# First batch entry's attention: exponentials transposed by TensorE, values with a column of ones, inputs loaded ahead

## The chip, the cores and the metric

The kernel runs on one NeuronCore of a Trainium2 chip. The metric is the device time of one execution in microseconds (us); of the kernel before, three runs were taken. The engines are named as the profile names them: PE (TensorE's matrix products) and PEld (its weight loads), DVE (VectorE), ACT (ScalarE), POOL (GpSimd) and SP (SyncE, which here only issues DMA transfers).

## What is computed

Windowed attention over 8 batch entries, 8 heads, 576 positions and 64 columns a head, and then a gated two-layer MLP on the 4608 tokens.

```python
scores = scale * np.matmul(q, k.transpose(0, 1, 3, 2))
rel = pos[:, None] - pos[None, :]
mask_plain = (rel >= 0) & (rel < window)                                   # window = 32
mask_dil = (rel >= 0) & (rel < window * dilation) & (rel % dilation == 0)  # dilation = 4
masks = np.stack([mask_plain if h < H // 2 else mask_dil for h in range(H)], axis=0)
scores = np.where(masks[None, :, :, :], scores, -1000000000.0)
attn = np.exp(scores - np.max(scores, axis=-1, keepdims=True))
attn = attn / (np.sum(attn, axis=-1, keepdims=True) + 1e-09)
x = np.matmul(attn, v)              # then (tokens, heads * columns) = (4608, 512)
h = x @ w_in                        # (512, 2048)
out = (h * (1.0 / (1.0 + np.exp(-1.702 * h)))) @ w_out
```

## The kernel before, in words

The MLP is done in nine groups of 512 tokens: one for the first 512 positions of each batch entry (`main`, tiles with `_m_` in their names) and one for the 64 positions that are left of all eight (`rest`). In a group, the 2048 hidden columns come in 16 blocks of 128. For block f, `up(f)` forms the hidden block on PE (12 products of 128x512, line 522), ACT takes a tanh (line 530), DVE multiplies the gate (line 533; called "gate f" below), and `down(f)` adds the block's share to four output banks (12 products, lines 558 to 562). Each operand is split into a high and a low fp32r part, and three products stand for one.

The weights lie in memory as 64-bit numbers. `decode(n)` brings one block of w_in or w_out (n = 0 to 31, even n for w_in, odd n for w_out) from there: a load of 512 KB into one of five cells (line 244), two ACT passes (lines 245, 246), one for the sign on ACT or DVE (238 or 240), two DVE passes (248, 250), a copy to the high part (ACT or DVE, lines 197 and 199) and a subtraction to the low part (DVE or POOL, line 204). All 32 blocks are decoded while the first main group runs.

A batch entry's attention is done in four head pairs k (k = 0 to 3 are the first entry, 4 to 7 the second). For a pair: `scores` (lines 328 and 337: the mask goes in by a product with the identity, then 76 products of 32 queries by up to 64 keys), `softmax` (lines 342 to 400: maximum, subtraction and exponential, sum, reciprocal, multiplication by it, a transposition of 32x32 blocks by DVE into `ct`, and eight copies of `ct` blocks into the banded tile `bt` by ACT, DVE or a DMA), `product` (line 414: `bt` by the values, 18 products whose result has the columns on the partitions), and `drain_x` (line 446 and on), which splits the result into `xh` (ACT) and `xl` (DVE), which `up` needs for all four pairs.

The order on each engine is fixed ahead of the run. All work is entered with `add(costs, urgency, work, reads, writes)`, and `Plan.ordered` places it by a list schedule: it takes the engine that can start first, on it the ready operation of lowest urgency, and the cheapest engine that may do it. Each engine then works through its list strictly in that order, and so does SP's queue of DMA issues. In the first 30 us of its own reckoning the plan fills PE's idle time with products of the identity (`warm`, line 630).

## Time and profile before

| | us |
|---|---|
| median of three runs | 918.69 (917.89 to 919.01) |
| the profiled execution, its own time | 920.26 |
| span of its profile | 918.5 |
| PE busy | 882.0 |
| DVE busy | 520.6 |
| ACT busy | 322.1 |
| POOL busy | 38.3 |

The profile is one execution; times in it count from the span's start. A share of the span mixes two stages: an early one, in which attention of the first entry and the decoding of the weights run, and a long one after it. A row of the timeline reads: start, duration, engine, line, operation, written tile <- read tiles, count, and in brackets how long the engine stood idle before and what ended that. A row of the table of stretches reads: stretch, its length, then busy time of PE, PEld, DVE, ACT and POOL (with instructions), the granted clock of PE as a share, the busy share of the DMA engines, GB/s.

### The profile page before, as it was taken

To read this page: it belongs to the slowest core of one execution; us is meant where nothing else is said; L and a number is where in the kernel's file an instruction comes from. 1 tells how busy PE (TensorE), PEld (TensorE's weight loads), DVE (VectorE), ACT (ScalarE), POOL (GpSimd) and SP (SyncE) were. 2 spreads that over 40 slices of the span, in tenths; PEclk is the share of its full clock that TensorE was granted. 3 is DMA by queue.
4 is the path that set the end of the run, shared out by engine and by line. 5 is a ranking of instruction groups with operands and counts; after the bars stand their busy time and mean duration, and the time that the engine had idled before them with its cause. 6 is when DMAs were issued, how large, how long until landed. Compare 5 with 4: busy or idle time off the path is not lost.

```text
span 918.5 us, 16806 instructions
## 1 busy us (share of the span) xinstructions
PE 882.0 (96%) x7096; PEld 718.5 (78%) x7096; DVE 520.6 (57%) x1004; ACT 322.1 (35%) x590; POOL 38.3 (4%) x40
## 2 busy tenths in 40 slices
PE   5679999999999999999999999999999999999997
PEld 2457778888888888888888888888888888888885
DVE  4878898676567636763667347654733433343332
ACT  2877887433344114321443134312421221121111
POOL 1121201000000000000000000000000000000000
PEclk9889999999999999999999999999999999999999
DMA  8566773323041102310222012300100010001002
GB/s 203 135 193 181 251 225 99 119 64 89 3 133 51 47 1 91 92 46 1 91 72 68 0 46 92 92 1 1 66 1 1 1 46 1 1 1 47 0 1 46
DMA packets 38683, 61.96 MB, mean 67 GB/s; under 512 B 20176, under 2 KB 20176, under 8 KB 38608
## 3 DMA queue, kind: packets, MB, share of 16 engines
q1 hardware_dynamic: 38608, 60.90, 22.1%
q8 instruction: 55, 0.90, 0.4%
q14 instruction: 20, 0.16, 0.1%
HBM read 49.81 MB, written 9.44 MB: 64 GB/s over the span
## 4 chain that ended last, share of the span: by engine, by line
PE 89%; DMA 4%; DVE 2%; ACT 2%; issue 0%; SPq 0%; ACTq 0%
PE hp_m L522 36%; PE acc_m L558 12%; PE acc_m L562 12%; PE acc_m L559 12%; PE hp_r L522 5%; PE av L414 4%; PE sp L337 3%; PE acc_r L562 2%; PE acc_r L558 2%; PE acc_r L559 2%; DMA cell<-wo_dram 1%; DMA qk<-qk_dram 1%; DMA bt<-ct 1%; DMA cell<-wi_dram 1%; ACT cell L238 0%
## 5 line engine op out<-in xcount | busy, mean ns | idle before, releaser
L522 PE MATMUL hp_m<-xh,wih 128*128 128x512 f32 x512 | 201.7, 394 | 7.1 <-DVE g_m L533 3.6
L533 DVE SCALAR_TENSOR_TENSOR g_m<-g_m,hp_m 128x512 f32<-128x512 f32 x128 | 87.8, 686 | 212.6 <-ACT g_m L530 211.9
L558 PE MATMUL acc_m<-gh,woh 128*128 128x512 f32 x512 | 201.0, 393 | 1.3 <-ACT gh L197 1.2
L522 PE MATMUL hp_m<-xh,wil 128*128 128x512 f32 x512 | 200.2, 391 | 0.7 <-DVE wil L204 0.7
L522 PE MATMUL hp_m<-xl,wih 128*128 128x512 f32 x512 | 200.1, 391 | 0.0
L559 PE MATMUL acc_m<-gh,wol 128*128 128x512 f32 x512 | 199.4, 389 | 0.0
L530 ACT ACTIVATE g_m<-hp_m 128x512 f32<-128x512 f32 x128 | 76.6, 598 | 308.2 <-PE hp_m L522 304.9
L562 PE MATMUL acc_m<-gl,woh 128*128 128x512 f32 x512 | 142.6, 391 | 0.0
L522 PEld LDWEIGHTS hp_m<-xh,wih 128*128 128x128 f32 x512 | 96.6, 189 | 29.5 <-DVE g_m L533 4.9
L558 PEld LDWEIGHTS acc_m<-gh,woh 128*128 128x128 f32 x512 | 96.1, 188 | 22.3 <-ACT gh L197 1.6
L522 PEld LDWEIGHTS hp_m<-xh,wil 128*128 128x128 f32 x512 | 96.6, 189 | 20.9 <-DVE wil L204 1.0
L522 PEld LDWEIGHTS hp_m<-xl,wih 128*128 128x128 f32 x512 | 96.5, 188 | 20.5
L562 PEld LDWEIGHTS acc_m<-gl,woh 128*128 128x128 f32 x512 | 95.7, 188 | 20.2
L559 PEld LDWEIGHTS acc_m<-gh,wol 128*128 128x128 f32 x512 | 96.1, 188 | 19.6
L204 DVE TENSOR_TENSOR gl<-g_m,gh 128x512 fp32r<-128x512 f32 x125 | 88.6, 709 | 15.7 <-ACT gh L197 7.2
L197 ACT ACTIVATE bt<-ct 32x320 f32<-32x320 f32 x109 | 51.1, 469 | 34.8 <-DVE ct L381 33.0
L199 DVE CAST gh<-g_m 128x512 fp32r<-128x512 f32 x106 | 45.3, 427 | 9.0 <-PE acc_m L559 0.5
L533 DVE SCALAR_TENSOR_TENSOR g_r<-g_r,hp_r 128x512 f32<-128x512 f32 x16 | 11.0, 688 | 54.4 <-ACT g_r L530 54.4
L197 ACT ACTIVATE xm<-av 128x512 f32<-128x512 f32 (+2 forms) x42 | 23.1, 613 | 52.9 <-PE av L414 35.0
L371 ACT ACTIVATE pr<-pr 128x640 f32<-128x640 f32 x32 | 23.7, 740 | 48.5 <-DVE pr L204 48.4
L199 DVE COPY bt<-ct 32x320 f32<-32x320 f32 x107 | 34.0, 318 | 2.4
L530 ACT ACTIVATE g_r<-hp_r 128x512 f32<-128x512 f32 x16 | 9.6, 598 | 73.4 <-PE hp_r L522 73.4
(129 smaller groups left out, 873.0 us busy)
## 6 DMA issues: line engine op xcount, KB each, us to landing
qk<-qk_dram SPq DMA_DIRECT2D x17, 576.0 KB, 5.1
out_dram<-ost_m SPq DMA_DIRECT2D x32, 256.0 KB, 2.1
second<-qk_dram SPq DMA_DIRECT2D x13, 576.0 KB, 4.7
v<-vp_dram SPq DMA_DIRECT2D x34, 216.0 KB, 4.5
cell<-wi_dram SPq DMA_DIRECT2D x11, 512.0 KB, 4.9
cell<-wo_dram SPq DMA_DIRECT2D x11, 512.0 KB, 4.0
words<-vp_dram SPq DMA_DIRECT2D x24, 216.0 KB, 4.2
second<-wi_dram SPq DMA_DIRECT2D x5, 512.0 KB, 5.1
```

Of the source, the lines that this page charges most:

```text
L197: A.activation(dst, src, AF.Copy, scale=scale)
L199: V.tensor_copy(out=dst, in_=src)
L204: (V if e == DVE else G).tensor_tensor(out=dst, in0=a, in1=b, op=op)
L337: T.matmul(dst[:, w:w + n], u["q"][rows, 32 * g:32 * g + 32], keys[:, at:at + n], start=not masked(k), stop=True, tile_position=(D * a, 32 ...
L371: add({ACT: 0.75}, urgency, lambda e: A.activation(pr, pr, AF.Exp, scale=0.125), (), (PR,))
L414: T.matmul(dst, u["v"][a][0:KW, m], bt[0:KW, a, m], start=True, stop=True, skip_group_check=True)
L522: T.matmul(hps[f], st[:, f, c], mv[:, c], start=c == 0 and k == 0, stop=c == NC - 1 and k == 2)
L530: A.activation(self.g32, hps[f], AF.Tanh, scale=0.851)
L533: V.scalar_tensor_tensor(out=self.g32, in0=self.g32, scalar=1.0, in1=hps[f], op0=ALU.add, op1=ALU.mult)
L558: T.matmul(self.acc[j], woh[:, f, cols], gh, start=f == 0, stop=False)
L559: T.matmul(self.acc[j], wol[:, f, cols], gh, start=False, stop=False)
L562: T.matmul(self.acc[j], woh[:, f, P * j:P * j + P], self.g[f][1], start=False, stop=f == NF - 1)
```

## The change

Only the first entry's four pairs (k = 0 to 3) are done in another way, and the plan's rules around them.

- Both heads' scores go to one bank, so maximum and subtraction are one DVE instruction of 640 columns each (before: two of 320 each). The exponentials are no longer summed, scaled or transposed by DVE. PE transposes them by products with a float identity (`exact`): ten products into `turned` and a spare bank (`turn`). ACT copies them to `ct`.
- PE multiplies `ct` by overlapping blocks of 64 values with a column of ones behind them (65 columns, 40 products, `times_values`). The last column is the sum. It is copied out, gets 1e-9 added and is inverted; DVE multiplies the 64 columns by it while it takes them out of the bank (two instructions), and PE transposes the result back (`turn_back`, five products). Then `drain_x` as before.
- The values of the first entry come as `vb`, one load of 128x1170 floats (585 KB) a pair in place of two of 216 KB. Queries, keys and values of the four pairs have places of their own (`bt`, `second`, `xm`, `xr`, `cell2`); the clearing of `bt` comes after that.
- In the plan: operations of the first entry that can start within 0.6 of another operation's cost go ahead of it (`AHEAD`), the first weights' loads go among the entry's loads, `up(1)` of the first group gets a bank of its own, and the `warm` products use another bank.

```diff
+            if e != DMA and ops[i][1][0] >= soon:
+
+                cost = min(abs(ops[i][0][k]) for k in ops[i][0])
+                near = [j for j in open_[e] if 0.0 <= ops[j][1][0] < soon and start(j, e) < when + AHEAD * cost]
+                if near:
+                    i = min(near, key=lambda j: (start(j, e), ops[j][1]))
+                    when = start(i, e)
...
-        early = ("pr0",) if n in (1, 2) else ()
-        add({DMA: 524}, urgency, lambda e: load(raw, src), early, (R, R + "l", *taken))
+        add({DMA: 524}, {0: -5.0, 1: -2.0}.get(n, urgency), lambda e: load(raw, src), (), (R, R + "l", *taken))
...
-        add({DMA: 590}, 1.6 * k - 2.0, work, waits(k), (place,))
+        add({DMA: 590}, (-9.0, -8.0, -6.0, -3.0)[k] if k < NC else 1.6 * k - 2.0, work, waits(k), (place,))
...
+                flat = (None, late, main_x, left_x)[k] if k else temp([P, nb], F32, "v", f"v_{k}")
+                u["v"] = flat[:, 0:nb].rearrange("p (g d) -> p g d", g=NB)
+                load(flat[:, 0:nb], vb[k])
...
     def first_attention(k, urgency):
...
-        softmax(k, urgency)
-        add({PE: 1.1}, urgency - 1.0e5, lambda e: product(k), (lots(k)[1], *(f"bt.{m}" for m in range(8))),
-            ("hp" if k % 2 else "av", f"spare{k}"))
+        exponentials(k, urgency)
+        def turn(e):
...
+            for t in range(QT):
+                n = min(P, S - P * t)
+                for a in range(2):
...
+                    T.matmul(dst, pr[0:n, a, t], exact[0:n, 0:n], start=True, stop=True, tile_position=(0, D * a),
+                             skip_group_check=True)
+        add({PE: 1.3}, urgency - 1.0e5, turn, (PR,), ("acc0", f"end{y}"))
+        add({ACT: 0.62}, urgency, lambda e: copy(e, ct[:, 0:GT], u["turned"]), ("acc0",), (CT + ".0", f"x{y}.0", f"x{y}.1"))
+        add({ACT: 0.22, DVE: 0.15}, urgency, lambda e: copy(e, ct[:, GT:], u["end"]), (f"end{y}",), (CT + ".1", f"x{y}.0", f"x{y}.1"))
+        def times_values(e):
...
+                    T.matmul(u["sums"][a][32 * j:32 * j + 32, t], ct[rows, 32 * g:32 * g + 32], u["v"][rows, g],
+                             start=True, stop=True, tile_position=(D * a, 32 * j), skip_group_check=True)
...
+            add({DVE: 0.17, ACT: 0.2}, urgency, lambda e, a=a: copy(
+                e, sm[:, a], u["sums"][a][:, :, D]), (f"acc{2 + a}",), (f"{SM}.{a}",))
...
+            add({DVE: 0.48}, urgency, lambda e, a=a: pair(
+                e, x[:, :, a], u["sums"][a][:, :, 0:D], sm[:, a, :, None].broadcast_to([P, QT, D]), ALU.mult),
+                (f"acc{2 + a}", SM, CT + ".0", CT + ".1"), (f"x{y}.{a}",))
+        def turn_back(e):
...
+                T.matmul(u["av"][:, P * t:P * t + n] if t < QT - 1 else u["rest"],
+                         x[0:n, t].rearrange("p a w -> p (a w)"), exact[0:n, 0:n], start=True, stop=True,
+                         skip_group_check=True)
...
-            place = "hp"
+            place = "sp" if self is main[0] and f == 1 else "hp"
...
+    keys = [f"bt.{m}" for m in range(8)]
+    add({POOL: 1.2}, 20.0, lambda e: G.memset(bt[0:KW], 0.0), (), ("first qk1", *keys))
```

**DVE between the second pair's `xl` and the third's.** Names: `pr`, `sm` are exponentials and sums of a pair, `words` and the cells belong to `decode`, `sums` is the new product's bank; line 250 of before is line 267 of after. Before:

```order
L250 ISA words<-cell_115,words 128x1024
L381 STREAM_TRANSPOSE ct_84<-pr_78 128x320 x2
L204 TENSOR_TENSOR xl<-av_408,xh 128x512
L199 COPY bt<-ct_84 32x10x32 x3
L372 TENSOR_REDUCE sm_83<-pr_79 128x10
L248 TENSOR_SCALAR words<-words 128x512
L373 TENSOR_SCALAR sm_83<-sm_83 128x10
L204 TENSOR_TENSOR wil<-words,wih 128x512
L376 RECIPROCAL sm_83<-sm_83 128x10
L250 ISA words<-cell_116,words 128x1024
L204 TENSOR_TENSOR pr_79<-pr_79,sm_83 128x320 x2
```

And after:

```order
L267 ISA words<-cell_118,words 128x1024
L222 TENSOR_TENSOR xl<-av_498,xh 128x512
L217 COPY ct_85<-spare 128x64
L520 TENSOR_SCALAR sm_82<-sm_82 128x10
L522 RECIPROCAL sm_82<-sm_82 128x10
L222 TENSOR_TENSOR ct_84<-sums_0_509,sm_82 128x5x64
L222 TENSOR_TENSOR ct_84<-sums_1_510,sm_82 128x5x64
L267 ISA words<-cell_116,words 128x1024
L265 TENSOR_SCALAR words<-words 128x512
L217 CAST woh<-words 128x512
L222 TENSOR_TENSOR xl<-av_571,xh 128x3x128
```

The sums (line 372), the transpositions (381) and the copies to `bt` (199) are gone from DVE; the second pair's `xl` now stands behind the decoding of a block in `cell_118`.

**PE around the start of the first group's products.** `hp_m_0` and `hp_m_1` are the banks of `up(0)` and `up(1)`, `av` a pair's result. Before, from the last pair's `product` on:

```order
L414 MATMUL av_527<-bt,xr 64x64
L414 MATMUL av_527<-bt,cell_117 64x64
L414 MATMUL idle<-bt,xr 64x64
L414 MATMUL idle<-bt,cell_117 64x64
L522 MATMUL hp_m_0_569<-xh,wih 128x512
L522 MATMUL hp_m_0_569<-xh,wil 128x512
L522 MATMUL hp_m_0_569<-xl,wih 128x512
```

And after, from the end of the second pair's `times_values` on:

```order
L512 MATMUL sums_1_422<-second,ct_85 32x65
L594 MATMUL hp_m_0_475<-xh,wih 128x512
L594 MATMUL hp_m_0_475<-xh,wil 128x512
L594 MATMUL hp_m_0_475<-xl,wih 128x512
L497 MATMUL turned_482<-early,pr_79 64x128 x8
L497 MATMUL spare<-early,pr_79 64x64 x2
L533 MATMUL av_498<-early,ct_85 128x128 x4
L533 MATMUL spare<-early,ct_85 128x64
```

The first group's products now begin between the pairs, and nine of the twelve of `up(1)` stand ahead of the last three of `up(0)`.

**SP's queue of loads at the start.** `qk`, `bt`, `second`, `xm`, `xr` and `cell` are the places that the loads fill. Before:

```order
L279 DMA xm<-qk_dram 128x1152
L297 DMA second<-vp_dram 96x576
L297 DMA xr<-vp_dram 96x576
L297 DMA xm<-vp_dram 96x576
L297 DMA xr<-vp_dram 96x576
L244 DMA cell_115<-wi_dram 128x512
L297 DMA xr<-vp_dram 96x576
L297 DMA cell_117<-vp_dram 96x576
L279 DMA qk_180<-qk_dram 128x1152
L395 DMA bt<-ct_84 32x10x32 x2
L244 DMA cell_116<-wo_dram 128x512
```

And after:

```order
L294 DMA second<-qk_dram 128x576
L295 DMA xm<-qk_dram 128x576
L261 DMA cell_116<-wi_dram 128x512
L312 DMA second<-vb_dram 128x1170
L294 DMA xr<-qk_dram 128x576
L295 DMA cell_118<-qk_dram 128x576
L261 DMA cell_117<-wo_dram 128x512
L312 DMA xm<-vb_dram 128x1170
L312 DMA xr<-vb_dram 128x1170
L261 DMA cell_116<-wo_dram 128x512
L261 DMA cell_118<-wi_dram 128x512
```

The first w_in block's load moved ahead of the second pair's values, the last pair's queries and keys no longer wait for the first pair's buffer, and the `bt` transfers are gone.

More of the change, by code (lines that the diff above doesn't have):

```diff
@@ L273, in work @@
         def work(e):
-            flat = {"qk0": None, "qk1": late, "qk2": main_x}[place]
-            if flat is None:
-                flat = temp([P, 2 * nq], F32, "qk", f"qk_{k}")
+            if k in (2, 3):
+                u["q"] = (late if k == 2 else left_x)[:, nb:nb + nq]
+                u["k"] = main_x[:, nb:nb + nq] if k == 2 else cell[:, 0:nq]
+                load(u["q"], qk[k, :, 0])
+                load(u["k"], qk[k, :, 1])
+                return
+            flat = windows if k == 1 else late if place == "qk1" else temp([P, 2 * nq], F32, "qk", f"qk_{k}")
             u["q"], u["k"] = flat[:, 0:nq], flat[:, nq:2 * nq]
@@ L297, in work @@
                 load(u["v"][a][0:KW], vp[k, :, a])
-        add({DMA: 442}, 1.6 * k - 0.3, work, waits(k), (place,))
+        add({DMA: 600 if k < NC else 442}, (-7.0, -4.0, -1.0, 0.0)[k] if k < NC else 1.6 * k - 0.3, work, waits(k),
+            (place,))
     def waits(k):
@@ L397, in work @@
                     copy(e, dst, src)
-            costs = ({DMA: 82} if NC <= k < FIRST * NC or k < NC and m % 4 == 3 else {ACT: 0.49, DVE: -0.33})
+            costs = {DMA: 82} if k < FIRST * NC else {ACT: 0.49, DVE: -0.33}
             add(costs, urgency, work, (f"{CT}.{prev}",), (f"bt.{m}",))
@@ L403, in product @@
         u = pairs[k]
-        u["av"] = bank([P, GT], "hp" if k < NC and k % 2 else "av", f"av_{k}")
-        if k < NC:
-            u["rest"] = spare_bank()[:, 1, LT * k:LT * k + LT]
-        else:
-            sp = pairs[k + 1]["sp"] if k + 1 < len(pairs) else bank([P, 2, GT], "sp", f"sp_{k + 1}")
-            u["rest"] = sp[:, 1, QT * W:QT * W + LT]
+        u["av"] = bank([P, GT], "av", f"av_{k}")
+        sp = pairs[k + 1]["sp"] if k + 1 < len(pairs) else bank([P, 2, GT], "sp", f"sp_{k + 1}")
+        u["rest"] = sp[:, 1, QT * W:QT * W + LT]
         for m in range(NW):
@@ L416, in spare_bank @@
     def spare_bank():
-        if not misc:
-            misc["bank"] = bank([P, 2, GT], "sp", "idle")
-        return misc["bank"]
+        if "spare" not in misc:
+            misc["spare"] = bank([P, GT], "acc1", "spare")
+        return misc["spare"]
     def drain_x(k, urgency):
         u, (b, c) = pairs[k], divmod(k, NC)
-        freed = ("qk2", "v2") if b == 1 else ()
+        freed = ("first v2", "first qk2") if b == 1 else ()
         def view(x):
@@ new lines, in first_attention @@
+        add({PE: 1.0}, urgency - 1.0e5, times_values, (lots(k)[1], CT + ".0", CT + ".1"), ("acc2", "acc3"))
+        x = cts[y].rearrange("p h a t q -> p (h a t q)").rearrange("p (t a w) -> p t a w", t=QT, a=2)
+        for a in range(2):
+            add({DVE: 0.17, ACT: 0.2}, urgency, lambda e, a=a: copy(
+                e, sm[:, a], u["sums"][a][:, :, D]), (f"acc{2 + a}",), (f"{SM}.{a}",))
+        add({DVE: -0.15}, urgency, lambda e: V.tensor_scalar(
+            out=sm, in0=sm, scalar1=1.0e-9, scalar2=None, op0=ALU.add), (f"{SM}.0", f"{SM}.1"), (SM,))
@@ new lines, in first_attention @@
+        add({DVE: 0.19}, urgency, lambda e: V.reciprocal(out=sm, in_=sm), (), (SM,))
+        for a in range(2):
+            add({DVE: 0.48}, urgency, lambda e, a=a: pair(
+                e, x[:, :, a], u["sums"][a][:, :, 0:D], sm[:, a, :, None].broadcast_to([P, QT, D]), ALU.mult),
+                (f"acc{2 + a}", SM, CT + ".0", CT + ".1"), (f"x{y}.{a}",))
+        def turn_back(e):
+            u["av"] = bank([P, GT], "av", f"av_{k}")
+            u["rest"] = spare_bank()[:, LT * (2 + k):LT * (3 + k)]
+            for t in range(QT):
+                n = min(P, S - P * t)
+                T.matmul(u["av"][:, P * t:P * t + n] if t < QT - 1 else u["rest"],
+                         x[0:n, t].rearrange("p a w -> p (a w)"), exact[0:n, 0:n], start=True, stop=True,
+                         skip_group_check=True)
@@ L475, in attention @@
             add({PE: 1.2}, urgency - 1.0e5, lambda e: scores(k), (lots(k)[0],),
-                ("sp", *(f"spare{j}" for j in range(NC))), 1.0)
+                ("sp",), 1.0)
         load_v(k)
@@ L628, in warm @@
     def warm(e):
-        if 0 not in main[0].hps and "sp" not in pairs[NC]:
-            T.matmul(spare_bank()[:, 0], ident, ident[:, None, :].broadcast_to([P, GT // P, P]), start=True, stop=True)
-    for work, e in plan.ordered(warm, WARM):
+        if 0 not in main[0].hps:
+            if "idle" not in misc:
+                misc["idle"] = bank([P, GT], "hp", "idle")
+            T.matmul(misc["idle"], ident, ident[:, None, :].broadcast_to([P, GT // P, P]), start=True, stop=True)
+    for work, e in plan.ordered(warm, WARM, NC):
         work(e)
@@ L652 @@
     vp[:, :, 32:] = order(v)
+    vb = np.ones((H, D, NB, DV), v.dtype)
+    vb[:, :, :, :D] = np.stack([vp[0, :, 32 * g:32 * g + D] for g in range(NB)], axis=2)
     vp = np.stack([vp[:, :, D * m:D * m + KW] for m in range(NW)], axis=2)
```

114 lines of the change are left out of this document (66 added, 48 removed).

## The prediction

> **What bounds the kernel now.** I read the table of stretches first, to see where PE stands idle.
>
> ```profile
> 0.00:20.00 20.00, 9.03 (x239) 4.83 (x240) 7.04 (x22) 3.48 (x5) 2.37 (x10) 1.00 0.90 209
> 20.00:54.84 34.84, 22.32 (x272) 14.07 (x270) 28.40 (x68) 28.35 (x51) 3.42 (x4) 0.80 0.63 173
> 54.84:119.09 64.25, 59.83 (x634) 47.40 (x634) 54.89 (x106) 50.62 (x77) 13.93 (x10) 1.00 0.67 205
> 119.09:155.25 36.16, 34.24 (x252) 27.95 (x252) 32.68 (x64) 30.92 (x52) 3.04 (x2) 1.00 0.54 159
> 155.25:175.25 20.00, 20.00 (x191) 16.50 (x190) 15.21 (x31) 9.11 (x18) 2.02 (x2) 1.00 0.38 127
> ```
>
> The last row is the long stage: PE busy 20.00 of 20, nothing else can shorten it. All that can be won lies ahead of it. There DVE and ACT are the full engines, not PE: in the second row 28.40 and 28.35 of 34.84. The edges of the rows are three of the sixteen "gates" of the first main group (line 533), which the timeline gives, with the first product of `up(0)`:
>
> ```profile
> 49.32 0.76 PE L522 MATMUL hp_m<-xh,wih 128*128 128x512 f32 x1 [3.07 <-DVE xl L204]
> 54.84 0.69 DVE L533 SCALAR_TENSOR_TENSOR g_m<-g_m,hp_m 128x512 f32<-128x512 f32 x1
> 155.25 0.68 DVE L533 SCALAR_TENSOR_TENSOR g_m<-g_m,hp_m 128x512 f32<-128x512 f32 x1
> 140.42 2.72 PE hp_m L522 x12
> ```
>
> The next rows price PE's attention: busy PE and count of line 414 (36 products), then of line 337 (76), in one stretch at full clock, and the two mask products.
>
> ```profile
> 23.00:26.60 3.60, 1.27 (x36) 1.13 (x36) 1.00 0.74 174
> 23.00:26.60 3.60, 1.00 (x76) 0.84 (x76) 1.00 0.74 174
> 23.75 0.43 PE L328 MATMUL sp_acc<-mask,ident 128*128 128x320 bf16 x2
> ```
>
> PE starts when the last `xl` is there. Twelve products take 2.72 at full pace (the row from the chain of waits). From gate 0 to gate 15 PE has 348 products to do (348 x 2.72 / 12 = 78.9 us) and the second entry's attention (four times 1.00 + 0.43 for scores and mask, 1.27 for the product: 10.8): 89.7, and takes 100.4. So some 10.7 us are lost there too, while DVE and ACT together work 169.1 of 200.8. From 20 us to gate 15 the two do 225.9 us of work in 135.25 us, 1.67 us a us. I take this sum of two engines' work as what sets gate 15; after it the order is the same.
>
> **What the change removes and adds on DVE and ACT.** The groups of 0 to 50 us:
>
> ```profile
> L197 ACT ACTIVATE bt<-ct 32x320 f32<-32x320 f32 x11 | 5.2, 468 | 0.3
> L199 DVE COPY bt<-ct 32x320 f32<-32x320 f32 x13 | 4.1, 317 | 0.3
> L362 DVE TENSOR_REDUCE mx<-sp_acc 128x5 f32<-128x320 f32 x8 | 3.8, 481 | 10.9 <-PE sp_acc L337 10.9
> L204 DVE TENSOR_TENSOR pr<-sp_acc,mx 128x320 f32<-128x320 f32 x8 | 3.8, 485 | 0.1
> L381 DVE STREAM_TRANSPOSE ct<-pr 128x320 f32<-128x320 f32 x8 | 3.6, 491 | 0.0
> L372 DVE TENSOR_REDUCE sm<-pr 128x10 f32<-128x640 f32 x4 | 3.3, 818 | 0.1
> L204 DVE TENSOR_TENSOR pr<-pr,sm 128x320 f32<-128x320 f32 x5 | 2.7, 567 | 0.0
> L197 ACT ACTIVATE xh<-av 128x512 fp32r<-128x512 f32 x2 | 1.2, 598 | 1.0 <-PE av L414 0.8
> 27.00 0.22 ACT L197 ACTIVATE xr<-idle 128x64 f32<-128x64 f32 x1
> 56.24 0.82 DVE L368 TENSOR_REDUCE mx<-sp 128x10 f32<-128x640 f32 x1
> 57.10 0.82 DVE L204 TENSOR_TENSOR pr<-sp,mx 128x640 f32<-128x640 f32 x1
> ```
>
> Gone are the first seven rows: 26.5 us. Maximum and subtraction come back as eight instructions of 0.82 (last two rows): 6.6. The multiplication by the inverse comes back as eight instructions of 128x320 out of a bank; nearest is the subtraction, 485 ns: 3.9. New are four copies of 128x512 out of a bank (598 ns: 2.4), four of 128x64 (0.22: 0.9) and eight of the sums, five columns each (at most 0.22, at least nothing: 1.8 or 0; I take 1.8, the row of the nearest size). Together 15.6. Net 10.9 us less; with the sums' copies at nothing it is 12.7.
>
> The rest comes from what the plan then gives to POOL. Up to gate 15 the order of after holds on DVE 16 low-part subtractions of weights for 22, 13 of `gl` for 12, 15 high-part casts for 19 (ACT 17 for 13), and 4 multiplications `pr<-pr,sm` for 8 in the second entry.
>
> ```profile
> L204 DVE TENSOR_TENSOR wol<-words,woh 128x512 fp32r<-128x512 f32 x10 | 6.9, 686 | 0.1
> L204 DVE TENSOR_TENSOR gl<-g_m,gh 128x512 fp32r<-128x512 f32 x12 | 8.4, 698 | 2.3 <-ACT gh L197 2.3
> L199 DVE CAST woh<-words 128x512 fp32r<-128x512 f32 x9 | 3.8, 417 | 0.1
> L197 ACT ACTIVATE woh<-words 128x512 fp32r<-128x512 f32 x5 | 3.2, 643 | 0.0
> ```
>
> That is -6 x 0.686 + 0.698 - 4 x 0.417 + 4 x 0.643 - 4 x 0.567 = -4.8. Its cover is POOL, busy 13.93 of 64.25 in the third stretch. Sum -15.7 us of work; over 1.67 that is **9.4 us earlier at gate 15**. What a block costs the two engines:
>
> ```profile
> L245 ACT ACTIVATE words<-cell 128x512 f32<-128x512 f32 x16 | 10.8, 677 | 3.0 <-DMA cell<-wo_dram 1.6 <-DMA cell<-wi_dram 0.8 <-DVE wol L204 0.6
> L246 ACT ACTIVATE cell<-cell 128x512 uint32<-128x512 uint32 x16 | 10.7, 678 | 2.4 <-DMA cell<-wi_dram 1.5 <-DMA cell<-wo_dram 0.8
> L238 ACT ACTIVATE cell<-cell 128x512 f16<-128x512 f32 x15 | 20.6, 1374 | 0.2
> L250 DVE CUSTOM_DVE_ANT_0 words<-cell,words 128x1024 uint16<-128x1024 uint16 x17 | 11.5, 676 | 0.0
> ```
>
> By gate 0 the queues hold 10.9 less but one more decoded block (six of line 250 for five): 0.68 + 0.68 + 1.37 + 0.68 and a cast of 0.42, 3.8. The 7.1 left, over the second stretch's own 1.63 us a us, is 4.3: gate 0 near 50.5. PE then has 94.9 us to gate 15 for 89.7 less the nine products of `up(1)` that already stand ahead (2.0): it fits.
>
> **PE.** It loses four times 18 products and gains 10 transposes of up to 128 columns, 40 products of 65 and 5 transposes back a pair. At half clock, line 414 in a later stretch:
>
> ```profile
> 43.90:46.30 2.40, 1.98 (x32) 1.82 (x32) 0.50 0.39 70
> ```
>
> That is 0.062 a product for 0.035 (1.27 / 36). The bounds at full clock: a transpose between 0.07 (two 64-column products) and 0.23 (a 512-column one, 2.72 / 12); a product of 65 between 0.013 (1.00 / 76) and 0.035. A pair then costs 1.6 to 4.9 in place of 1.27; I take 2.5, since each transpose fills only a quarter of 512 columns. It lies in PE's idle 12.5 us of the second stretch and costs nothing; without that cover four pairs would cost 1 to 15.
>
> The granted clock matters for that:
>
> ```profile
> 40.00:42.00 2.00, 0.00 (x0) 0.00 (x0) 1.97 (x6) 1.98 (x3) 0.00 (x0) 0.50 0.29 117
> 52.00:54.00 2.00, 2.00 (x7) 1.39 (x5) 1.45 (x3) 1.37 (x3) 0.00 (x0) 0.67 0.93 303
> 18.90 5.01 PE L630 MATMUL idle<-ident 128*128 128x512 bf16 x14
> 27.27 2.10 PE L630 MATMUL idle<-ident 128*128 128x512 bf16 x9 [0.69 <-ACT xr L197]
> ```
>
> After PE's idle time around 40 the clock is 0.50 and returns only during 52 to 54, four us after the products began at 49.32. The filling products ran at 0.36 each from 18.90 and at 0.23 from 27.27. The change takes out nearly all of them (40 become 4 in the order). [...]
>
> **Loads.** The values grow by 153 KB a pair, 0.63 MB together, ahead of the weights.
>
> ```profile
> 14.00:16.00 2.00, 1.13 (x63) 0.91 (x63) 0.00 (x0) 0.62 (x1) 0.00 (x0) 1.00 1.07 229
> 18.45 0.53 PE L337 MATMUL sp_acc<-xm 64*32 64x64 f32 x13 [2.43 <-issue]
> 21.06 0.67 ACT L245 ACTIVATE words<-cell 128x512 f32<-128x512 f32 x1 [6.44 <-DMA cell<-wi_dram]
> 24.38 0.33 PE L337 MATMUL sp_acc<-qk 64*32 64x32 f32 x14 [0.20 <-DMA qk<-qk_dram]
> ```
>
> In the first 20 us the DMA engines are full at 229 GB/s, so 0.63 MB is 2.8 us for what stands behind. The first w_in block landed at 21.06; it now has 2.9 MB up to its end instead of 3.6 ahead in the queue and lands some 3 us sooner. The last pair's scores began at 24.38, with PE waiting only 0.20 for them: "all at once" gives little. In the later stretches DMA is busy 0.54 to 0.67, which hides the 2.8; uncovered, it costs 2.8. POOL's moved clearing of `bt` waits for a read of it and nobody waits on POOL then.
>
> **Sum.** The profiled execution took 920.26 (span 918.5 and 1.76 around it): 920.26 - 9.4 = 910.9. The median of the runs is 1.57 lower, so I predict **909.3**.
>
> **Rivals.**
>
> *PE's floor.* If the lead on DVE and ACT also ends the 10.7 us lost after gate 0 (at gate 10 the order has three pairs' softmax behind it in before, two after), gate 15 comes 4.3 + 10.7 + 2.0 = 17 us earlier: 901.7. Against it: the two engines would have to do 1.8 us a us, which only the fourth stretch (1.76) came near. 0.13.
>
> *Late inputs.* The lists are fixed, and first-pair work stands behind weights that may land late: ACT's second exponential behind the first w_in block, the second pair's `xl` on DVE behind `cell_118`, whose load is the sixteenth or so in a full queue (6.9 MB: 33 us at 229 GB/s, and 3 more as the 21.06 row lagged). If half the gain goes in such waits: 914. For it: 6.44 above, and the 2.43 in which PE had nothing to execute that the trace shows. 0.17.
>
> *Half clock.* A pair at half clock costs 1.6 to 4.9 more, and one pair, the last, is on the path; 24 products of `up(0)` and `up(1)` at 0.43 for 0.23 cost 4.8, of which before pays 2. In all 4.4 to 7.7 on 909.3: 913.7 to 917.0, about 915. [...] Against it: PE's list is dense from about 25 us on, which restored the clock in 52 to 54. 0.08.
>
> *Nothing moves.* The gates wait for something that the change leaves as it is. A load's landing ended only 0.20 at PE above. 0.05, 918.7.
>
> *Slower: the weights' loads become the bound.* If each block is late by the extra 2.8 us and the wait is not caught up, the time is 918.7 + 2.8 = 921.5. It decides from the point where ACT's waits for landed cells (lines 245 and 246 above, 55 to 155 us: 1.6 + 0.8 + 1.5 + 0.8 = 4.7) grow by more than the 9.4 won. A DMA share of 0.67 speaks against it. 0.07.
>
> **The numbers.** The forecast, 6 to 12 us better, has 0.50. Faster by over 0.2% (1.8 us, about what a measurement of this kernel can tell from no change) is the forecast and the first three rivals: 0.88; within it 0.05; slower 0.07. The range leaves out the slower end and no change, and the outer half of the PE floor: 901 to 917.
>
> **What would show it.** Right: line 372 four times fewer and no DVE transposes before gate 0; gate 0 near 50.5, gate 15 near 146, DVE and ACT still near 1.67 us a us between, PE saturated after it. Wrong: ACT idle on `cell` for over 10 us before gate 0 (late inputs); `hp_m` products at 0.43 beyond 24 of them, or a clock of 0.50 past 50 us (half clock); gate 15 ahead of 140 (PE's floor); gate 15 at 155 in spite of less DVE work (another bound).

## The result, and the profile after

The changed kernel takes 907.07 us (median of 4 runs, 906.11 to 908.55), the kernel before 918.29 (4 runs, 917.87 to 919.01): a ratio of 0.9878, 95% interval 0.9861 to 0.9896, or 11.2 us less. The forecast was 909.3. The profiled execution of the changed kernel took 906.11 (span 904.4); it is the fastest of its four, while that of before (920.26) is 2.0 above the median of 918.29, so the two profiles lie 14.1 apart, 2.9 more than the medians do, and differences between profiles below are to be read with that.

The table of stretches of the changed kernel, with edges at its gates 0, 10 and 15 and 20 us beyond:

```profile
0.00:20.00 20.00, 12.45 (x349) 7.71 (x349) 9.09 (x25) 7.15 (x10) 2.84 (x12) 1.00 0.82 292
20.00:46.86 26.86, 21.57 (x431) 16.63 (x431) 19.45 (x45) 21.47 (x48) 3.65 (x3) 0.94 0.59 190
46.86:107.13 60.27, 57.60 (x526) 46.30 (x527) 52.63 (x98) 52.48 (x80) 16.70 (x14) 1.00 0.67 200
107.13:141.02 33.89, 33.60 (x351) 26.82 (x349) 30.00 (x55) 30.15 (x52) 7.04 (x6) 1.00 0.62 186
141.02:161.02 20.00, 20.00 (x191) 16.54 (x190) 15.19 (x31) 9.13 (x18) 2.01 (x2) 1.00 0.42 134
```

PE is again busy all the time after gate 15. DVE and ACT (third and fourth of the busy times) did 9.09 + 7.15 = 16.2 us of work in the first 20 us, where before they did 7.04 + 3.48 = 10.5. The timeline of the changed kernel has the edges, and what PE and ACT do on the way:

```profile
14.19 0.65 ACT L262 ACTIVATE words<-cell 128x512 f32<-128x512 f32 x1
27.85 0.50 PE L594 MATMUL hp_m<-xh,wih 128*128 128x512 f32 x1
28.97 1.09 PE L497 MATMUL turned<-early,pr 128*64 128x128 f32 x16
30.26 1.16 PE L533 MATMUL av<-early,ct 128*128 128x128 f32 x8
31.71 1.04 PE L512 MATMUL sums<-xm,ct 64*32 64x65 f32 x80
44.32 0.50 PE L594 MATMUL hp_m<-xh,wih 128*128 128x512 f32 x1 [2.74 <-ACT xh L215]
46.86 0.68 DVE L605 SCALAR_TENSOR_TENSOR g_m<-g_m,hp_m 128x512 f32<-128x512 f32 x1
141.02 0.67 DVE L605 SCALAR_TENSOR_TENSOR g_m<-g_m,hp_m 128x512 f32<-128x512 f32 x1
```

Gate 0 stands 8.0 us earlier (54.84 before), gate 15 14.2 earlier (155.25). ACT starts on the first w_in block at 14.19, waiting for nothing; before, at 21.06 after 6.44 idle. The first product of `up(0)` runs at 27.85 (49.32 before). From gate 15 to the end are 763.4 us in both kernels (918.5 - 155.25 = 763.3, 904.4 - 141.02 = 763.4): gate 15 carries the whole difference.

The groups of 0 to 50 us of the changed kernel have the prices of the new steps, which came as the forecast took them (0.825 for 0.82, 0.485, 0.602 for 0.598), and the blocks decoded by then (line 267):

```profile
L267 DVE CUSTOM_DVE_ANT_0 words<-cell,words 128x1024 uint16<-128x1024 uint16 x7 | 4.8, 684 | 0.5 <-ACT cell L256 0.3
L222 DVE TENSOR_TENSOR ct<-sums,sm 128x320 f32<-128x320 f32 x8 | 3.5, 485 | 0.3
L374 DVE TENSOR_REDUCE mx<-sp 128x10 f32<-128x640 f32 x4 | 3.3, 825 | 9.1 <-PE sp L355 9.1
L215 ACT ACTIVATE ct<-turned 128x512 f32<-128x512 f32 x4 | 2.4, 602 | 5.3 <-PE turned L497 5.3
```

The same view of the kernel before:

```profile
L250 DVE CUSTOM_DVE_ANT_0 words<-cell,words 128x1024 uint16<-128x1024 uint16 x4 | 2.7, 671 | 0.1
```

Seven blocks for four. DVE's largest wait is for PE's scores (9.1) as it was before (10.9).

**The theory and its rival.** The forecast's theory: the summed work of DVE and ACT sets gate 15, so what is taken from them shortens it at 1.67 us a us. It fits the profile only when a second thing is counted, how much of that work is already done early. The split at 50 us shows it, before first:

```profile
0.00:50.00 50.00, 26.89 (x498) 15.87 (x499) 33.24 (x85) 28.75 (x51) 5.78 (x14) 0.90 0.72 174
50.00:155.25 105.25, 98.53 (x899) 78.39 (x898) 89.78 (x173) 84.61 (x133) 16.96 (x12) 0.98 0.64 194
```

And the changed kernel:

```profile
0.00:50.00 50.00, 36.43 (x790) 26.33 (x791) 31.67 (x74) 31.73 (x63) 6.49 (x14) 0.97 0.70 233
50.00:141.02 91.02, 88.79 (x866) 71.13 (x864) 79.50 (x146) 79.52 (x127) 23.74 (x19) 1.00 0.64 194
```

Up to gate 15 there are 236.4 us of work before and 222.4 after, of which 62.0 and 63.4 are done by 50 us: the changed kernel has less to do and yet had done more. The rivals were that loads and the first entry's chain of steps set gate 0 (whatever the work), and that the plan's rules, not the lighter attention, are what counts.

### The profile page after: what moved, and what is told of

It is laid out like the page before. It is cut to its first block, busy times and chain, and to the rows that moved or that the text cites. A ratio compares the mean times of both kernels' runs of the same rounds, so it can differ in the third digit from the quotient of the medians.

```text
span 904.4 us, 17292 instructions
## 1 busy us (share of the span) xinstructions
PE 881.3 (97%) x7356; PEld 721.8 (80%) x7356; DVE 508.7 (56%) x966; ACT 319.9 (35%) x595; POOL 45.8 (5%) x47
## 4 chain that ended last, share of the span: by engine, by line
PE 94%; ACT 3%; DVE 1%; DMA 1%; issue 0%; SPq 0%; DVEq 0%; ACTq 0%
PE hp_m L594 38%; PE acc_m L630 13%; PE acc_m L634 12%; PE acc_m L631 12%; PE hp_r L594 5%; PE sp L355 3%; PE av L428 3%; PE acc_r L634 2%; PE acc_r L630 2%; PE acc_r L631 2%; PE turned L497 1%; DMA qk<-qk_dram 1%; DMA cell<-wo_dram 0%; ACT second L256 0%; ACT cell L256 0%
## 5 line engine op out<-in xcount | busy, mean ns | idle before, releaser
L215 ACT ACTIVATE bt<-ct 32x320 f32<-32x320 f32 x98 | 46.0, 469 | 34.8 <-DVE ct L398 33.4
L217 DVE COPY bt<-ct 32x320 f32<-32x320 f32 x94 | 29.9, 318 | 2.1
```

Of the source, the lines that this page charges most:

```text
L215: A.activation(dst, src, AF.Copy, scale=scale)
L217: V.tensor_copy(out=dst, in_=src)
```

## The experiments

Each was run in five rounds against the kernel before on its chip, in three sets; the kernel before took 917.82, 919.01 and 917.40 in them (17, 17 and 28 runs). Ratios are therefore compared, and a difference between two ratios is given in us of 918.3. With intervals of about 0.0018 to each side, two kernels less than some 2.3 us apart are not told apart by times alone.

### Are the loads' shapes a part of it?

**Values on 128 partitions in the kernel before** (`e1_before_v128`): the first entry's value loads fill 128 partitions, the last 32 with zeros.

```diff
-                load(u["v"][a][0:KW], vp[k, :, a])
+                n = P if k < NC else KW
+                load(u["v"][a][0:n], vp[k, 0:n, a])
```

> The kernel before, with one edit: the first entry's value loads fill 128 partitions (zeros in the last 32) in place of 96; same count, 288 KB for 216 KB each, same order of everything. Work theory (the gain comes only from DVE and ACT work that is gone, about 14 us at 1.67 us a us): no work is gone, so no change, 918.3 within 0.5; more bytes could cost up to 1. Load theory (part of the gain comes from loads that fill all 128 partitions and so move faster): GB/s over the first 20 us rises from 209 towards 292, the first w_in block reaches ACT near 16 us in place of 21.06, and the time falls by 1 to 3.4 us, to 915 to 917.3.

Measured: 916.42 us, ratio 0.9986 (0.9975 to 0.9996), 1.3 us less. In the stretches of 6 to 18 us, the kernel before and then this one:

```profile
6.00:18.00 12.00, 5.30 (x209) 3.45 (x209) 4.36 (x10) 1.47 (x2) 0.00 (x0) 1.00 1.03 236
```

```profile
6.00:18.00 12.00, 8.87 (x231) 4.84 (x232) 7.87 (x19) 3.07 (x5) 0.00 (x0) 0.80 0.94 363
```

Both times the DMA engines are full (1.03, 0.94); the last column is what they move: 236 GB/s and 363. A full DMA share is no measure of the bytes here. With it ACT's first w_in block started 4.7 us sooner than in the kernel before (21.06):

```profile
16.38 0.67 ACT L245 ACTIVATE words<-cell 128x512 f32<-128x512 f32 x1 [3.41 <-DMA cell<-wi_dram]
```

This is the nearest that the runs come to earlier weights in the kernel before, and it brought 1.3 us. PE's granted clock was lower at the same time (half for some 23 of the first 50 us, counted in stretches of 1 us, for 10 before), so what the loads alone are worth there is not separated.

**Values as two halves in the changed kernel** (`e2_after_v64`):

```diff
-                load(flat[:, 0:nb], vb[k])
+                for rows in (slice(0, D), slice(D, P)):
+                    load(flat[rows, 0:nb], vb[k, rows])
```

> The changed kernel, with one edit: each of the four value loads is issued as two loads of 64 partitions; same bytes, same order of everything else. Work theory: no change, 907.1 within 0.7. Load theory: the rate of 400 GB/s between 6 and 18 us falls towards the 212 that both kernels show at 2 to 6 us, when the first pair's queries and keys come in two halves of 64 partitions; the first w_in block comes 2 to 5 us later and the time rises by 1 to 3.4 us, to 908 to 910.5.

Measured: 910.93 us, ratio 0.9925 (0.9906 to 0.9944), 4.3 us more than the changed kernel. The same stretch, changed kernel and then this one:

```profile
6.00:18.00 12.00, 10.12 (x335) 7.04 (x335) 5.31 (x8) 4.41 (x6) 1.16 (x1) 1.00 1.02 403
```

```profile
6.00:18.00 12.00, 8.23 (x266) 5.69 (x272) 3.95 (x6) 3.22 (x6) 1.16 (x1) 0.93 1.03 252
```

And its waits of PE up to 50 us and the first block on ACT:

```profile
PE turned L498 <- issue: 4.8, 1, 4.8
PE sp L356 <- issue: 2.9, 1, 2.9
```

```profile
16.08 0.66 ACT L262 ACTIVATE words<-cell 128x512 f32<-128x512 f32 x1 [2.41 <-DMA cell<-wi_dram]
```

Full engines at 252 GB/s instead of 403; the first block comes 1.9 us later, and PE's waits marked "issue", in which it waited for nothing that the profile shows, are 7.7 us instead of 2.8. It cost more than was expected (3.4 at most). That second wait grew too, and PE's granted clock was 0.50 to 0.56 from 16 to 30 us, where the changed kernel is low (0.54 to 0.61) only from 22 to 26; the shares of the two were not separated. So the shape is a part of the gain, the smaller one in the kernel before (1.3), a larger one in the changed kernel, where more hangs on the first 20 us.

**The first queries and keys in one load** (`e9_after_qk128`), where both kernels use two halves of 64 partitions:

```diff
-            for rows in (slice(0, D), slice(D, P)) if k == 0 else (slice(0, P),):
+            for rows in (slice(0, P),):
```

> The changed kernel, with the first pair's queries and keys in one load of 128 partitions in place of two of 64; same order of everything else. Load theory: 2 to 6 us runs near 400 GB/s in place of 213, the scores end about 1 us sooner, and the time falls by 0.5 to 1.2. Work theory: the same work, started by a chain that is not the bound: 0 to 0.3 less. Against both: two halves let the first half's scores begin sooner (PE begins at 5.05 now), so up to 0.5 more.

Measured: 905.13 us, ratio 0.9863 (0.9844 to 0.9882), 1.4 us less than the changed kernel: in the direction expected, within the uncertainty. The load ran faster, 2 to 6 us of the changed kernel and then of this one:

```profile
2.00:6.00 4.00, 1.62 (x14) 0.44 (x12) 1.51 (x8) 0.82 (x3) 0.51 (x3) 1.00 0.96 213
```

```profile
2.00:6.00 4.00, 2.12 (x75) 1.12 (x77) 1.51 (x8) 0.81 (x3) 0.52 (x3) 1.00 0.95 351
```

**The last two pairs' values later** (`e12_after_v_late`), and **both edits** (`e13_after_qk128_v_late`), to see whether PE's long wait marked "issue" (2.40 us in the changed kernel) goes when less is loaded:

```diff
-        add({DMA: 600 if k < NC else 442}, (-7.0, -4.0, -1.0, 0.0)[k] if k < NC else 1.6 * k - 0.3, work, waits(k),
-            (place,))
+        add({DMA: 600 if k < NC else 442}, (-7.0, -4.0, -1.0, 0.0)[k] if k < NC else 1.6 * k - 0.3, work,
+            ["pr1"] if k in (2, 3) else waits(k), (place,))
```

> The changed kernel with one edit: the value loads of the third and fourth pair (585 KB each) wait for the second pair's exponentials, so that 1.2 MB leave the queue of the first 20 us. Up to the first product of the gated layer the order on every engine is the same. Theory A (PE's 2.40 us without instructions at 18.2 to 20.6 us is its instructions being fetched behind the bulk loads, and the wait lies on the path to gate 0): the stall falls below 1 us, gate 0 comes 1.5 to 2 us earlier, 905.0 to 905.6. Theory B (the stall is no matter of the loads, or something else is late just behind it): stall and gate 0 stay, 907.1; if the late values themselves are then waited for, 908 to 909.

> The changed kernel with the edits of two runs together: the first pair's queries and keys in one load over 128 partitions (alone 1.9 us better), and the third and fourth pair's values waiting for the second pair's exponentials. If both lie on one chain from the first load to gate 0 (theory A of the run with late values), the gains add: 903.2 to 903.7, gate 0 near 43. If the stall of PE's instructions takes back what the earlier start gives, or doesn't depend on the loads: 905.1, as with the one load alone.

Measured: 908.35 us, ratio 0.9882 (0.9863 to 0.9902), and 905.63, ratio 0.9857 (0.9838 to 0.9876): what the changed kernel and the one with whole queries and keys have without the edit. Theory A fell as it stood. In the first one's stretch the loads of the weights simply moved up:

```profile
6.00:18.00 12.00, 10.02 (x334) 6.72 (x315) 6.08 (x12) 4.84 (x7) 1.16 (x1) 1.00 1.00 391
```

The queue stayed full (1.00, 391 GB/s) and the stall 2.9 us long, 2.4 in the second kernel. What the stall waits for is not settled by these times; the last section has what the traces show beside it.

### Does the work of DVE and ACT set the gates?

**Four more reductions early** (`e3_after_more`), one behind each subtraction of the first entry:

```diff
+            if k < NC:
+                V.tensor_reduce(out=mx.rearrange("p a t -> p (a t)"),
+                                in_=exact[:, None, 0:W].broadcast_to([P, 2 * QT, W]), axis=AX.X, op=ALU.max)
```

> The changed kernel, with four more DVE reductions of 128x640 (0.82 us each, of a constant into a tile whose value is no longer needed), one behind each first-entry subtraction; same order of everything else. Work theory: 3.3 us of work at 1.70 us a us, 1.9 us more: 909.0. Chain theory (in the first 47 us a chain through PE, DVE and ACT sets the pace, and DVE has idle time that hides them): 0 to 0.8 more. If each stands on the chain: 3.3 more, 910.4.

Measured: 907.40 us, ratio 0.9888 (0.9868 to 0.9907), 0.9 more by the ratio, 0.3 by the medians: too close to either for a verdict from the times. Its stretches show where the dose went:

```profile
0.00:50.00 50.00, 35.40 (x786) 25.38 (x787) 33.76 (x76) 30.73 (x61) 6.52 (x14) 0.93 0.66 233
50.00:141.97 91.97, 89.81 (x871) 72.07 (x870) 80.49 (x150) 80.62 (x128) 23.73 (x19) 1.00 0.64 191
```

Up to gate 15 there is 225.6 us of work (3.2 more than in the changed kernel), but of 50 us 64.5 are used (1.1 more): a third of the dose filled time in which DVE waits for scores anyway. The 2.1 that were left over cost 0.95 at gate 15.

**Twelve more reductions between the gates** (`e14_after_more_later`), in the decoding of blocks 10 to 21:

```diff
+            if 10 <= n < 22:
+                V.tensor_reduce(out=unused, in_=ident[:, None, 0:W].broadcast_to([P, 2 * QT, W]), axis=AX.X,
+                                op=ALU.max)
```

> The changed kernel with twelve more DVE reductions over 640 columns (0.82 us each in this kernel, 9.8 us in all), one in the decoding of each of the blocks 10 to 21, between gate 0 and gate 15; every other instruction stands in the same order. Theory of the forecast (DVE and ACT's summed work sets the distance of the gates): 9.8 over 1.75 us a us is 5.6 us, 912.7, gate 15 at 146.6. Rival (PE sets that stretch, and DVE has slack): 907.1 to 908.6, gate 15 at 141.0 to 142.5. Rival (DVE alone is the bound there, not the sum): up to 9.8 us, 917.

Measured: 909.99 us, ratio 0.9904 (0.9887 to 0.9922), 2.4 us more than the changed kernel; 12 x 0.80 = 9.6 us of work were added. The two stretches:

```profile
0.00:50.00 50.00, 37.12 (x787) 26.39 (x788) 32.11 (x75) 32.23 (x63) 6.76 (x15) 0.91 0.68 235
50.00:144.28 94.28, 90.61 (x870) 72.08 (x869) 87.02 (x158) 79.58 (x126) 23.77 (x19) 0.99 0.61 186
```

Gate 15 came 3.3 us later, between the 5.6 of the forecast's theory and the 0 to 1.5 of a stretch that PE sets. Both seem to be part of it: PE's idle time from 50 us to gate 15 grew from 2.2 (91.02 - 88.79) to 3.7, and the two engines went from 1.75 us a us to 1.77. Of DVE's work in the changed kernel, a microsecond costs a quarter to a third there, not 0.57.

**The kernel before without sum and scaling** (`e7_before_nosum`), and **without transpositions and copies** (`e15_before_nobt`); both leave part of the first entry's attention out:

```diff
-        add({DVE: 0.80}, urgency, lambda e: V.tensor_reduce(out=sm, in_=pr, axis=AX.X, op=ALU.add), (PR,), (SM,))
+        add({DVE: 0.80}, urgency, lambda e: k >= NC and V.tensor_reduce(out=sm, in_=pr, axis=AX.X, op=ALU.add), (PR,), (SM,))
...
-            add({DVE: 0.42}, urgency, lambda e, half=half: V.transpose(
+            add({DVE: 0.42}, urgency, lambda e, half=half: k >= NC and V.transpose(
```

(The addition, reciprocal and multiplication likewise in the first, the copies to `bt` in the second.)

> The kernel before, leaving out sum, addition of 1e-9, reciprocal and scaling of the first entry's exponentials (its first 512 positions of output are not normalised); every other instruction stands in the same order. DVE loses 7.5 us of work and POOL three multiplications, all ahead of gate 0. Theory of the forecast (the summed work of DVE and ACT sets the gates): 7.5 over 1.63 us a us is 4.6 us at gate 0, 913.2. Chain theory (what counts is the way from the loads over a pair's steps to gate 0): of the last pair 0.82 + 0.17 + 0.21 + 2 x 0.57, about 2.3 us, and little from the earlier pairs, which run behind the loads: 915.0 to 916.0. If the loads alone set gate 0: 917 to 917.8.

> The kernel before, leaving out the 32x32 transpositions by DVE and all the copies from ct to bt (on DVE, ACT and by DMA) of the first entry, so that its products multiply the cleared bt (that entry's first 512 positions come out as zeros); every other instruction stands in the same order. DVE loses 7.7 us of work, ACT 5.2, and PE's waits for bt (4.4 on DVE, 3.1 on DMA) go. Theory of the forecast (summed work): 12.9 over 1.63 is 7.9 us, 911. Scaled by what leaving out the 7.5 us of sums, reciprocals and scaling gave (2.4 us by the ratio, 0.32 us a us): 4.1 us, 914 to 915. If only the last pair's way counts (two transpositions of 0.49 and about two copies, 1.8 us): 917.

Measured: 916.02 us, ratio 0.9974 (0.9961 to 0.9986), 2.4 us less for 7.5 of work; and 915.64, ratio 0.9977 (0.9964 to 0.9991), 2.1 us less for 12.9. Both far from 4.6 and 7.9. In both, ACT's first block also started sooner than before (17.98 and 18.42 for 21.06), so that even this gain is not that of less work alone. The second one's stretches:

```profile
0.00:50.00 50.00, 30.51 (x586) 18.66 (x586) 28.41 (x70) 26.51 (x46) 5.78 (x14) 0.90 0.68 204
50.00:148.72 98.72, 92.76 (x809) 74.51 (x810) 86.68 (x168) 80.81 (x127) 16.98 (x12) 1.00 0.62 188
```

Its work up to gate 15 is 222.4 us, to the tenth what the changed kernel has. But by 50 us only 54.9 of it are done, not 63.4: more than half of the 12.9 us that were taken away left DVE and ACT idle, and the weights that could have filled the gap were not there yet (ACT waited 4.2 us for its first block, and started it at 18.42). Less work is worth little where nothing else is at hand.

### Are the plan's rules and the early weights what counts?

**The new attention with all old rules** (`e17_after_oldplan`):

```diff
-AHEAD = 0.6
+AHEAD = 0.0
...
-        add({DMA: 524}, {0: -5.0, 1: -2.0}.get(n, urgency), lambda e: load(raw, src), (), (R, R + "l", *taken))
+        early = ("pr0",) if n in (1, 2) else ()
+        add({DMA: 524}, urgency, lambda e: load(raw, src), early, (R, R + "l", *taken))
...
-            place = "sp" if self is main[0] and f == 1 else "hp"
+            place = "hp"
```

> The changed attention and its loads with the old rules of the plan: no going ahead (AHEAD = 0), the first weights' loads where the kernel before had them, up(1) in the bank that the other blocks use. The order changes on every engine from the second pair on. If the gain is that of the work that the attention no longer gives to DVE and ACT, and of its loads over 128 partitions: 907 to 909. If the plan's rules carry a good part (the 4.8 us of work that went to POOL, and products of up(1) ahead): 910 to 913. If the old rules even suit it: 905 to 906.

**Only the weights' loads late** (`e5_after_late_w`: the second piece of that diff alone):

> The changed kernel with the first two weights' loads back where the kernel before had them, behind the entry's loads. ACT's first block, which starts at 14.19 us in the changed kernel, starts later by the 1.7 MB that then stand ahead, about 4 us at 400 GB/s, near 18 us; ACT loses up to 4 us of early work. Summed work: 4 over 1.7 is 2.4 us, 909.5. If the entry's own loads are what counts, they come 1.2 us sooner for the second pair's values and later: 906 to 907.

**Only the going ahead off** (`e4_after_ahead0`: its first piece alone):

> The changed kernel with AHEAD = 0: operations of the first entry no longer go ahead of work on the weights that can start a little earlier. If the way of the pairs to gate 0 sets the time, each such operation now waits behind a piece of decoding (0.68 to 1.37 us on ACT, 0.4 to 0.7 on DVE), a few times on that way: gate 0 later by 2 to 4 us, 909 to 911. If the summed work sets it (the same work in another order): 907.1. If the rule costs more than it gives: 905 to 906.

| kernel | us | ratio to before (95%) | above the changed kernel |
|---|---|---|---|
| all old rules | 914.22 | 0.9969 (0.9956 to 0.9982) | 8.4 |
| weights' loads late | 913.46 | 0.9957 (0.9939 to 0.9974) | 7.3 |
| no going ahead | 910.71 | 0.9922 (0.9907 to 0.9938) | 4.0 |

The first two are the largest effects of the study. With the old rules the new attention and its loads are 2.8 us better than the kernel before (0.18% to 0.44%); putting back the loads of two weight blocks alone costs 7.3, nearly all of the other 8.4. The three do not add up (going ahead alone is 4.0 of them, and the three together are 8.4), as would be so if they fill the same idle time or cost the same clock. The stretches with late weights:

```profile
0.00:50.00 50.00, 35.17 (x770) 25.76 (x771) 25.45 (x62) 23.49 (x51) 5.61 (x13) 0.83 0.56 195
50.00:149.81 99.81, 95.35 (x884) 75.73 (x883) 86.28 (x163) 86.90 (x139) 23.37 (x17) 0.98 0.65 201
48.00:50.00 2.00, 2.00 (x5) 1.61 (x6) 1.93 (x6) 2.00 (x5) 0.00 (x0) 0.50 0.97 316
```

And its count of decoded blocks up to 50 us:

```profile
L268 DVE CUSTOM_DVE_ANT_0 words<-cell,words 128x1024 uint16<-128x1024 uint16 x5 | 3.5, 693 | 1.4 <-ACT cell L256 1.4
```

222.1 us of work again, but 48.9 of it by 50 us. The 14.5 that are missing there, at the changed kernel's 1.75 us a us, make 8.3 us; gate 15 came 8.8 us later (149.81). ACT's first block started at 21.91 instead of 14.19, more than the 4 us expected. The expected loss (4 us of ACT's early work, 2.4 us of time) was too small: the second and third block came at 32.89 and 34.04 instead of 21.78 and 29.32, so that both engines lost time, and not by the first block alone.

Late data was hardly what they waited for: up to 60 us ACT waited 0.6 us for a cell. The plan had put the rest of the decoding behind steps of the pairs, and these waited for PE (ACT 3.11 us up to 25.69, 3.69 up to 29.98), which ran almost without a break at half clock:

```profile
24.00:26.00 2.00, 2.00 (x10) 1.78 (x9) 1.67 (x3) 0.31 (x1) 0.00 (x0) 0.50 0.61 186
26.00:28.00 2.00, 2.00 (x86) 1.71 (x87) 0.36 (x2) 0.29 (x1) 0.00 (x0) 0.50 0.23 84
28.00:30.00 2.00, 1.93 (x20) 1.41 (x16) 0.40 (x1) 0.02 (x1) 0.00 (x0) 0.51 0.73 219
```

From 20 to 50 us the mean granted clock is 0.73 in this kernel and in the one with all old rules, as of some 16 us at half clock, and 0.94 in the changed kernel, as of some 4. The time of its eleven runs goes with the mean granted clock, too: five runs with 0.990 to 0.992 took 910.87 to 913.46, six with 0.985 to 0.987 took 913.14 to 916.58 (the profile, 915.43, is one of these). Against the kernel before, the five are 5.7 us better by their median, and the changed kernel's two runs with 0.991 and 0.992 are 10.2 us better. By this estimate from few runs some 4.5 of the 7.3 us remain at an equal clock, and the rest goes with the clock. Whether the late loads brought the lower clock about was not tested. All old rules:

```profile
0.00:50.00 50.00, 34.21 (x765) 24.99 (x765) 27.43 (x65) 25.13 (x51) 4.33 (x12) 0.83 0.57 195
50.00:150.58 100.58, 98.14 (x895) 78.13 (x895) 86.06 (x164) 83.67 (x137) 18.63 (x15) 0.96 0.65 200
```

222.3 us, 52.6 of them by 50 us. Four kernels with the same work of DVE and ACT up to gate 15 (222.1 to 222.4) thus have it at 141.02, 148.72, 149.81 and 150.58, the changed kernel alone with over 60 us done by 50. Among the other three the order isn't that of the early work, since the rates after 50 us differ (1.70, 1.74, 1.69). PE can be read for the same stretch: with all old rules it had done 9 products of the first group by 50 us, the changed kernel 34, and then was busy for 98.14 us up to gate 15 instead of 88.79, with 2.4 us idle for 2.2. Nearly all of the 9.6 us by which gate 15 is later there is PE's own work and its half clock up to some 57 us (0.50 from 50 to 56, 0.71 from 56 to 58).

Without the going ahead the picture is another:

```profile
0.00:50.00 50.00, 35.68 (x780) 25.10 (x780) 31.69 (x79) 31.91 (x62) 5.22 (x13) 0.96 0.67 229
50.00:142.40 92.40, 91.29 (x800) 73.88 (x801) 78.59 (x154) 77.28 (x116) 12.14 (x9) 0.97 0.59 182
50.00:52.00 2.00, 0.89 (x2) 0.50 (x2) 2.00 (x5) 2.00 (x4) 0.00 (x0) 0.50 1.02 405
52.00:54.00 2.00, 2.00 (x6) 1.60 (x5) 2.00 (x5) 1.93 (x5) 0.00 (x0) 0.50 0.96 286
```

DVE and ACT did as much by 50 us (63.6) as in the changed kernel. Here PE is behind: a granted clock of 0.50 from about 49 to 56 us, where the changed kernel has 1.00: one product of 128x512 follows another after 0.43 us there (at 54.14 and 54.57), and after 0.23 once the clock is back (at 56.24 and 56.47). Gate 15 came only 1.4 us later, though (142.40). From there to the end are 766.5 us (908.9 - 142.40) instead of 763.4, because scores and product of one pair more of the second entry (2.6 us of PE, from 142.11 on) lie there, and PE stood idle for 0.7 us at 150.5. So gate 15 does not carry the difference in this kernel; how much of the 4.0 is the clock and how much the order was not separated.

## Why the prediction was right, and where it wasn't

**The number and its reason.** 909.3 was forecast, 907.07 came, in the range. The forecast's "I take this sum of two engines' work as what sets gate 15" can be filled in as measured: the work up to gate 15 fell by 14.0 us (15.7 forecast), worth 8.4 at 1.67; 5.7 us more of it was done in the first 20 us, worth 3.4; and from 20 us on the rate was 1.70 instead of 1.67 (206.2 us in 121.0), worth 2.4. Together 14.2, gate 15's shift in the profiles (the medians differ by 11.2). That this closes is arithmetic, since work divided by time is the rate in any kernel; it does not show that the sum sets the gate. The experiments speak against the price: 9.6 us of work more between the gates cost 2.4 to 3.3 us and not 5.6, and 7.5 and 12.9 less ahead of gate 0 brought 2.4 and 2.1 and not 4.6 and 7.9. From 50 us to gate 15 PE is the fullest engine of the changed kernel, busy 98% (88.79 of 91.02) where DVE and ACT are at 87% each, so that the two engines' work seems to count there as far as it keeps PE waiting. (Two slips of the working bear on nothing: from gate 0 at 50.5 to gate 15 at 145.8 are 95.3 us and not 94.9, and 6.9 MB at 229 GB/s take 30 us and not 33.)

**The mis-sized term: the first 20 us.** The forecast took them as unchanged. "The first w_in block ... lands some 3 us sooner" was seen, but got no term in the sum, and "all at once gives little" dismissed the rest. The block started 6.9 us earlier, and putting the two early loads back costs 7.3 us, a part of it through PE's clock. Gate 0 moved by 8.0 for 4.3. Behind it stands "the DMA engines are full at 229 GB/s": full they were, but while the values, 0.63 MB larger, came in, the same full engines moved 403 GB/s, so that the 2.8 us priced for them were not paid.

**The attribution.** The main term, 10.9 us less work for DVE and ACT in the attention, was priced at 1.67 us a us, 6.5 us, and is hardly worth that by itself: under the old rules attention and loads together bring 2.8 (with PE at half clock for longer, as above). Leaving work out of the kernel before brought 0.32 and 0.16 us a us. A rate taken from a stretch in which two engines are mostly busy holds for work that is done there only if other work steps into its place. Here the early weights and the order of the plan made that work available. That the sum came out near the result is in part luck: the left-out gain of the loads and the overpriced gain of the attention stood against each other. The early loads of the weights alone were not tried in the kernel before; values on 128 partitions brought its first block 4.7 us forward for 1.3 us, so the loads do not seem to be worth 7.3 without the rest.

**PE.** A pair's new products take 3.8 us at full clock (from 28.97 to 32.75; 1.09 + 1.16 + 1.04 and 0.76 for those into the spare bank), for 2.5 taken and 4.9 as the upper bound, and lay in idle time: between 20 and 46.86 us PE still had 5.3 us idle (26.86 - 21.57). The low price has a reason: the kernel issues 38 products for a pair's scores and 18 for its `product`, and the profile lists each of them twice, 76 and 36 (as it lists the 40 new ones as x80). The forecast and the description of the kernel took 76 for the number of products, so that one of 65 columns was priced from 0.013; it took 1.04 / 40 = 0.026.

**The rivals.** *Late inputs*: wrong; ACT started its first block without a wait, and up to 60 us waited 0.2 us for cells. *Half clock*: wrong for the changed kernel; that its attention would run at half clock throughout was the author's estimate, and from 20 to 46.86 us its mean granted clock was 0.94. It was low only here,

```profile
22.00:24.00 2.00, 2.00 (x80) 1.83 (x59) 1.09 (x2) 1.97 (x3) 0.00 (x0) 0.61 0.24 51
24.00:26.00 2.00, 2.00 (x17) 1.55 (x14) 1.59 (x3) 0.40 (x1) 0.00 (x0) 0.54 0.73 246
```

and one pair's products lay there, though a clock of 0.50 did hit experiments, from 20 us on and around gate 0. The filling products at 0.36 and 0.23, which the forecast set beside the clock, both ran at a granted clock of 1.00. *PE's floor*: half right; PE's idle time from 50 us to gate 15 fell from 6.7 to 2.2 us, without "against it", the rate of 1.8, being reached (1.75). *The weights' loads become the bound*: wrong; from 50 us to gate 15 ACT's waits for cells are 0.2 us and this one:

```profile
ACT cell L263 <- DMA cell<-wo_dram: 3.0, 1, 3.0
```

for 4.7 before. *Nothing moves*: wrong.

## What to carry to other kernels

Work taken from an engine shortened the early stage here only as far as other work was there to fill the gap (7.5 and 12.9 us left out brought 2.4 and 2.1), so ask of each freed microsecond what the engine will do instead, and whether its inputs have landed by then; here putting two loads back in a queue cost 7.3 us, while the rewritten attention under the old rules was worth 2.8. Before such a cost is laid to the loads, read the granted clock beside it: by the estimate above 2.8 of the 7.3 went with PE's clock. Count a stage's work as a sum, but also how much of it is done by a fixed early time: kernels of equal work differed by up to 9.6 us, most of it through that and through PE's clock. And of a full DMA queue read the bytes moved as well as the busy share, since here the same 12 us at a full share moved 236 GB/s with loads of 96 partitions and 363 with 128.
